# Gated mix of two linear-attention layers: a later clear for the feature weights, a fold half a V step later, and an earlier reload

## The chip, the cores and the metric

The kernel runs on one core of one Trainium2 chip. The metric is device microseconds of one execution; each comparison is the median of several runs. The core has five engines with a queue each: TensorE (PE in the profile, with its weight loads as PEld), VectorE (DVE), ScalarE (ACT), GpSimd (POOL) and SyncE (SP, which here issues nearly all DMAs). Each engine works through its own queue in order.

## The reference

Two linear-attention layers A and B read the same input x (2048 tokens, 448 features, 16 heads of 28) and are mixed by a gate:

```
def _A_ref(x, wqkv, w_phi, wo):           # _B_ref is the same with B's weights
    q, k, v = split(x @ wqkv)             # 16 heads of 28
    pq, pk = q @ w_phi, k @ w_phi         # per head, 28 x 28
    phi_q = concat(softmax(pq), softmax(-pq));  phi_k likewise
    kv = sum_s phi_k^T v;  z = sum_s phi_k
    o  = (phi_q @ kv) / (phi_q @ z + 1e-6)
    return o @ wo
g = sigmoid((x * gate_w).sum(-1))
out = g * A(x) + (1 - g) * B(x)
```

## The kernel before

**Tiles.** The 2048 tokens are 16 tiles of 128, loaded in 8 pairs. x arrives transposed, in 4 chunks of 128 feature rows. Every float32 factor is split in a high part, rounded by ACT, and a low part, the remainder, which DVE or POOL subtracts. A projection of one tile for one layer ("a half") is 11 matmuls of up to 450 columns: 4 chunks high x high, 4 high x low, 3 low x high. The letters V, K and Q name the projections: V into banks VA and VB, K into K0 and K1 and Q into Q. In the first step, V01, tiles 0 and 1 go chunk by chunk as their x and weights arrive.

**Fold.** The feature map w_phi is multiplied into the K and Q weights once, at the start. `load_wp` clears a tile wp, loads w_phi into it with eight small DMAs from POOL's queue, and subtracts its last column into wpd. Four folds F (0 to 3; layer A's two, then layer B's) multiply wpd with the raw weights wts (loaded from in_wkt and in_wqt) into the bank tile F, which there is once. After each fold DVE transposes F to SBUF (into ret for folds 0 and 2, into ru for 1 and 3; line 366), ACT rounds the high parts rk (for K) and rq (for Q), and DVE or POOL subtracts the low parts. The next fold may write F only when the transpose has read it. POOL's copy on line 350 fills a rest of wts ahead of each fold.

**Attention.** For each tile the K features are two softmaxes (ACT, DVE, POOL), and `kv` accumulates phi_k^T v for two tiles at a time in bank T (line 504). The Q features go from the bank (DVE subtracts the maximum into ru) to DRAM (qd, four DMAs of a tile) and back in another layout, then through softmaxes and a transpose into a "slot" eT. Tiles 0 to 7 are done early and spilled to DRAM (ed); tiles 8 to 15 are made just in time.

**End.** After the last kv block, N blocks (line 587) multiply phi_q of two tiles with kv; the first takes tiles 8 and 9 from slots 0 and 1, the second tiles 0 and 1 from slots 2 and 3, which `fetch` reloads from ed. Slots 2 and 3 lie in `ret` where the K features of the last tiles were, so a reload may begin only when the last kv block has read them. The gate for tiles 12 to 15 goes through DRAM (gd) into `gate` with four small DMAs. O blocks (line 635) are the output projections.

**Order.** `steps()` is the work in the order written by hand; TensorE follows it exactly. `Plan` collects every instruction as a step with an engine, an estimated cost, what it reads and writes as keys (r, w), and an `ahead` that makes it more urgent. `order()` then places the steps of the other engines, the most urgent ready step first, by those estimates. A key in r orders steps in the plan; on the chip an instruction waits for real data alone.

Of the kernel before, what the change touches and what calls it, by code (L numbers as in the profile page):

```python
# [13 lines left out]
P = 128  # L14
# [13 lines left out]
class Plan:  # L28
# [79 lines left out]

def steps():

    yield from (("V01", 0, 0, 1), ("x1",), ("V01", 1, 0, 1), ("wt", 0), ("wt", 1), ("x", 2), ("wt", 2), ("wt", 3), ("V", 2, 0), ("F", 0, "DP"), ("V", 2, 1))
    yield from (("V", 3, 0), ("F", 1, "NP"), ("V", 3, 1), ("F", 2, "DP"), ("V", 4, 0), ("F", 3, "DP"), ("x2",), ("later",), ("V", 4, 1), ("k", 0, 0), ("q", 0, 0), ("k", 0, 1), ("ks", 0))
    yield from (("K", 1), ("wo_rows",), ("q", 0, 1), ("qf", 0))
    yield from (("S", 0, JIT % 3 - 1), ("K", 2), ("Q", 1), ("S", 1, (JIT - 1) % 3 - 1), ("k", 3, 0), ("k", 3, 1), ("vm", 5, 0), ("kv", 0, 1), ("vo", 5, 0), ("ks", 3), ("V", 5, 1))
    for p in range(2, 7):
        yield "x", p + 1
        yield "K", 2 * p
        yield "Q", 2 * p - 2
        if 2 * p - 2 < JIT:
            yield "S", 2 * p - 2, (JIT - 2 * p + 2) % 3 - 1  # L120
        yield "kv", 2 * p - 2, 2 * p - 1
        yield "wo", p - 2
        if p == 3:
            yield "wo", 6
        if p < 6:
            yield "V", 2 * p + 2
        yield "K", 2 * p + 1
        yield "Q", 2 * p - 1
        if 2 * p - 1 < JIT:
            yield "S", 2 * p - 1, (JIT - 2 * p + 1) % 3 - 1  # L130
        if p < 6:
            yield "V", 2 * p + 3
        if p == 6:
            yield "gates", 0, 12
            yield "gates_b", 0, 12
    yield from (("K", 14), ("V", 14, 0), ("k", 15, 0), ("k", 15, 1), ("kv", 12, 13), ("wo", 5), ("load_wo",), ("Q", 12), ("ks", 15), ("V", 14, 1), ("V", 15, 0), ("Q", 13))
    yield from (("V", 15, 1), ("free_v",), ("free_k",), ("kv", 14, 15), ("free_e",), ("kv_turn",), ("gates", 12, NT))
    yield from (("fetch", 0, 2), ("fetch", 1, 3), ("Q", 14))
    kept, late = list(range(2, JIT - 2)), list(range(JIT, NT))
    rest = []  # L140
    while kept or late:
        rest.append((kept.pop(0) if kept else late.pop(0), late.pop(0) if late else kept.pop(0)))
    pairs = [((JIT - 1, JIT - 2), (0, 1)), ((0, 1), (2, 3))] + [(t, (2 * (i % 2), 2 * (i % 2) + 1)) for i, t in enumerate(rest)]
    for p, (tiles, slots) in enumerate(pairs):
        yield "num", tiles, slots
        if p == 0:
            yield from (("Q", 15), ("free_x",), ("free_q",))
        if p:
# [18 lines left out]
def hedgehog_mix(ctx: ExitStack, tc: tile.TileContext, xd, wv, wkt, wqt, wphi, wo, cmask, cpmask, out):  # L167
# [100 lines left out]
    def dma(o, i):  # L268
        return lambda: nc.sync.dma_start(o, i)  # L269
# [14 lines left out]
    raws = {p: (x1raw, "x1raw") if p == 1 else (xraw, "xraw") for p in range(NP)}  # L284

    def load_x0():
        for c in range(4):
            add("SP", 0.4, dma(xraw[:, c], xd[c * P:c * P + P, :2 * P]), [], [("x0raw", c)], lat=3 if c == 0 else 2, kb=131, ahead=9000.0 - 1000 * c)
            load_wv(c, 0)

    def split_x0():
# [38 lines left out]
        low_part(low, D, l, wvr[:, c, lo:hi], h.bitcast(F32), [("wvr", c, b), ("vh", c, b)], [("vl", c, b)], ahead=700.0 - 100 * c if b == 0 else 0.0)  # L330

    def load_wp():
        add("DVE", 0.15, lambda: V.memset(wp, 0.0), [], [("wp", q) for q in range(4)])
        for q in range(4):
            for b in range(2):
                i = wphi[:, b, q].rearrange("(g d) f -> d g f", g=4)
                add("POOL", 0.6, lambda q=q, b=b, i=i: G.dma_start(wp[32 * q:32 * q + DH, b], i), [("vh", 2, 0)], [("wp", q)], lat=3, two=False)
# [176 lines left out]
    def q_front(k):  # L514
        mx, km, uq, ku = qmx[k % 2], ("qmx", k % 2), uqs[k % 2], [("u", k % 2, b) for b in range(2)]

        def p4():
            return fm(bank["Q"][:, :, FO:FO + D])
        put("DVE", 2 * D, lambda: V.tensor_reduce(mx, p4(), AX.X, OP.max), ["Q"], [km])
        for b in range(2):  # L520
            put("DVE", D + 60, tt("DVE", uq[:, :, b], lambda b=b: p4()[:, b].rearrange("p (r g) f -> p r g f", r=4),
                                  mx[:, b].rearrange("p (r g) -> p r g", r=4)[:, :, :, None].to_broadcast([P, 4, 4, DH]), OP.subtract),
                ["Q", km], [ku[b]])
        m = qd[k]
        for c in range(4):
            add("SP", 0.4, dma(m[:, :, c].rearrange("r t x -> t r x"), uq[32 * c:32 * c + 32].rearrange("p r b g f -> p r (b g f)")),
                ku, [("qd", k, c)], lat=2.2, kb=160)

    def q_soft(k, slot):
        i = k % 2  # L530
# [27 lines left out]
    def gates(lo, hi):  # L558
        gl = glog[:, lo:hi]
        kl = [("gl", t) for t in range(lo, hi)]  # L560
        add("DVE", 0.1, lambda: V.tensor_scalar(gl, gl, 1.0, None, op0=OP.add), [], kl)
        add("DVE", 0.2, lambda: V.reciprocal(gl, gl), [], kl)
        add("SP", 0.4, dma(gd[:, lo:hi], gl), kl, [("gd", lo)], lat=2)
        for r in range(4):
            add("SP", 0.4, dma(gate[32 * r:32 * r + 32, 0, :, lo:hi], gd[:, lo:hi].rearrange("(c t) n -> t c n", c=4)), [("gd", lo)], [("ga", lo, r)], lat=2)

    def gates_b(lo, hi, after=()):
        add("POOL", 0.25, lambda: G.tensor_scalar(gate[:, 1, :, lo:hi], gate[:, 0, :, lo:hi], -1.0, 1.0, op0=OP.mult, op1=OP.add),
# [254 lines left out]
```

## Time and profile before

| | us |
|---|---|
| median of 3 runs | 339.39 (338.52 to 340.2) |
| the profiled execution | 338.98 |
| its span, first to last instruction | 337.2 |
| TensorE busy | 330.2 (98% of the span) |
| VectorE busy | 281.3 (83%) |
| GpSimd busy | 250.8 (74%) |
| ScalarE busy | 146.0 (43%) |

The granted TensorE clock was 0.998 of full speed. In the lines of a timeline the first number is the start in us from the start of the span, the second the duration, then engine, line, operation, destination<-sources, shapes and a count (neighbouring instructions of one kind are merged); in brackets the idle time before, and what ended it. A DMA's row is its issue, not its transfer. In a table of stretches each engine has its busy us with its number of instructions, then the granted clock, the DMA share and GB/s.

### The profile page before, as it was taken

To read this page: it belongs to the slowest core of one execution; us is meant where nothing else is said; L and a number is where in the kernel's file an instruction comes from. 1 tells how busy PE (TensorE), PEld (TensorE's weight loads), DVE (VectorE), ACT (ScalarE), POOL (GpSimd) and SP (SyncE) were. 2 spreads that over 40 slices of the span, in tenths; PEclk is the share of its full clock that TensorE was granted. 3 is DMA by queue.
4 is the path that set the end of the run, shared out by engine and by line. 5 is a ranking of instruction groups with operands and counts; after the bars stand their busy time and mean duration, and the time that the engine had idled before them with its cause. 6 is when DMAs were issued, how large, how long until landed. Compare 5 with 4: busy or idle time off the path is not lost.

```text
span 337.2 us, 8906 instructions
## 1 busy us (share of the span) xinstructions
PE 330.2 (98%) x3742; PEld 295.8 (88%) x3742; DVE 281.3 (83%) x339; ACT 146.0 (43%) x239; POOL 250.8 (74%) x210
## 2 busy tenths in 40 slices
PE   8999999999999999999999999999999999999994
PEld 7977899998999999999999999998778898888894
DVE  3648879799797896969899989796999999999860
ACT  4747845463264462524436244522133434433231
POOL 7118769999999979989896999693368868887300
PEclk9999999999999999999999999999999999999999
DMA  7983046532297857646556231855974454231011
GB/s 202 272 224 105 2 128 191 160 119 56 74 325 244 256 170 215 202 166 218 195 156 245 73 109 28 299 221 124 366 276 137 167 199 164 63 147 55 31 54 56
DMA packets 29904, 54.74 MB, mean 162 GB/s; under 512 B 4664, under 2 KB 25512, under 8 KB 27560
## 3 DMA queue, kind: packets, MB, share of 16 engines
q1 hardware_dynamic: 29608, 54.06, 49.5%
q8 instruction: 29, 0.48, 0.6%
q0 software_dynamic: 256, 0.12, 0.2%
q14 instruction: 11, 0.09, 0.1%
HBM read 31.54 MB, written 24.22 MB: 165 GB/s over the span
## 4 chain that ended last, share of the span: by engine, by line
PE 73%; DVE 10%; DMA 8%; POOL 4%; SPq 2%; issue 2%; ACT 1%; POOLq 0%; DVEq 0%; ACTq 0%
PE O L635 21%; PE K L419 14%; PE Q L419 11%; PE VA L419 8%; PE VB L419 7%; PE N L587 6%; POOL ret L263 3%; PE T L504 3%; DMA ret<-ed 2%; SPq L269 2%; DVE sm L492 2%; DMA rk<-wod 2%; DMA ret<-in_wv 1%; PE F L361 1%; PE K L451 1%
## 5 line engine op out<-in xcount | busy, mean ns | idle before, releaser
L419 PE MATMUL Q<-rq,rx 128*128 128x432 f32 x352 | 72.1, 359 | 0.0
L419 PE MATMUL K<-rk,rx 128*128 128x432 f32 x352 | 71.8, 359 | 0.0
L635 PE MATMUL O<-rk,rx 128*128 128x448 f32 x336 | 70.7, 368 | 0.4 <-issue 0.4
L635 PEld LDWEIGHTS O<-rk,rx 128*128 128x128 f32 x336 | 62.5, 188 | 8.8 <-issue 2.9
L419 PEld LDWEIGHTS Q<-rq,rx 128*128 128x128 f32 x352 | 65.8, 188 | 3.7 <-DVE ru L263 0.4
L419 PEld LDWEIGHTS K<-rk,rx 128*128 128x128 f32 x352 | 66.1, 188 | 3.1
L266 ACT ACTIVATE ret<-ret 128x896 f32<-128x896 f32 x48 | 45.6, 950 | 50.5 <-POOL ret L263 50.3
L263 POOL TENSOR_TENSOR ret<-ret,sm 128x896 f32<-128x896 f32 x32 | 53.9, 1704 | 2.4 <-DVE sm L493 2.2
L492 DVE TENSOR_REDUCE sm<-ret 128x32 f32<-128x896 f32 x32 | 33.9, 1071 | 6.5 <-ACT ret L266 6.5
L550 DVE STREAM_TRANSPOSE ret<-ret 128x2048 f32<-128x2048 f32 x16 | 36.5, 2283 | 0.8 <-POOL ret L263 0.5
L263 POOL TENSOR_TENSOR ret<-pk,mx 128x896 f32<-128x896 f32 x16 | 27.3, 1705 | 10.7 <-DVE mx L485 10.6
L545 DVE TENSOR_REDUCE qsm<-ret 128x32 f32<-128x896 f32 x32 | 33.3, 1060 | 1.6 <-ACT ret L266 1.5
L419 PE MATMUL VA<-rv,rx 128*128 128x450 f32 x154 | 34.3, 370 | 0.0
L419 PE MATMUL VB<-rv,rx 128*128 128x448 f32 x154 | 33.9, 367 | 0.0
L266 ACT ACTIVATE ret<-ru 128x896 f32<-128x896 f32 x16 | 15.3, 954 | 42.3 <-issue 20.0
L263 POOL TENSOR_TENSOR ret<-qmn,ru 128x896 f32<-128x896 f32 x16 | 28.2, 1761 | 7.2 <-DVE ret L550 4.2
L419 PEld LDWEIGHTS VB<-rv,rx 128*128 128x128 f32 x154 | 28.6, 188 | 3.5 <-issue 0.8
L419 PEld LDWEIGHTS VA<-rv,rx 128*128 128x128 f32 x154 | 28.7, 189 | 2.9 <-ACT rk L266 0.4
L263 POOL TENSOR_TENSOR ret<-ret,qsm 128x896 f32<-128x896 f32 x16 | 27.3, 1704 | 0.9
L263 POOL TENSOR_TENSOR ret<-mx,pk 128x896 f32<-128x896 f32 x16 | 27.3, 1704 | 0.7 <-DVE mx L486 0.7
L539 DVE TENSOR_REDUCE qmn<-ru 128x32 f32<-128x896 f32 x16 | 17.1, 1067 | 11.3 <-DMA ru<-qd 11.2
L607 POOL TENSOR_TENSOR rv<-rv,rd 128x896 f32<-128x896 f32 x14 | 23.9, 1704 | 1.1
(91 smaller groups left out, 448.5 us busy)
## 6 DMA issues: line engine op xcount, KB each, us to landing
ed<-ret SPq DMA_DIRECT2D x8, 1024.0 KB
ret<-ed SPq DMA_DIRECT2D x8, 1024.0 KB
qd<-ru SPq DMA_DIRECT2D x64, 112.0 KB
ru<-qd SPq DMA_DIRECT2D x16, 448.0 KB
out<-ret SPq DMA_DIRECT2D x16, 224.0 KB
wod<-wst SPq DMA_DIRECT2D x14, 224.0 KB
rk<-wod SPq DMA_DIRECT2D x2, 1568.0 KB
xraw<-in_xt SPq DMA_DIRECT2D x5, 512.0 KB
```

What stands on the lines that cost most here:

```text
L263: return lambda: ENG[eng].tensor_tensor(val(o), val(a), val(b), op)
L266: return lambda: A.activation(val(o), val(i), f, **k)
L269: return lambda: nc.sync.dma_start(o, i)
L419: nc.tensor.matmul(bank[name][:, k, lo:hi], x[:, xc, o:o + P], w[l][:, c], start=i == 0, stop=i == len(XT) - 1)
L492: put("DVE", 2 * D, lambda s=s, e3=e3: V.tensor_reduce(sm[:, s], e3, AX.X, OP.add), [ke[s], *([("u", 0, 1)] if t == 15 else [])], [("sm", ...
L504: nc.tensor.matmul(kvp()[32 * r:32 * r + DH + 1, b, g], vs[t % NV][:, b, h // 2, h % 2], es[t % NE][:, :, hs:hs + DH], start=(t == 0 and b ...
L539: put("DVE", 2 * D, lambda: V.tensor_reduce(qmn, tq.rearrange("p c b g f -> p c (b g) f"), AX.X, OP.min), [kt, *late], [kn])
L545: put("DVE", 2 * D, lambda s=s, e3=e3: V.tensor_reduce(qsm[:, s], e3, AX.X, OP.add), [ke[s], *late], [("qsm", i, s)])
L550: add("DVE", 2.25, lambda: V.transpose(eTf[slot], eq.rearrange("p s a c f -> p (s a c f)")), ke, turned(slot))
L587: nc.tensor.matmul(bank["N"][32 * g:32 * g + 32, r, 2 * b * P:2 * b * P + 2 * P], kvt[32 * r:32 * r + 32, b, s, g], eTp[slots[0] // 2][32 ...
L607: put(eng, 2 * D, lambda: ENG[eng].tensor_tensor(mid["o", n % 3].rearrange("p (c a f) -> p a c f", c=4, a=8), ctv()[:, :, i, :, :DH], rd[: ...
L635: nc.tensor.matmul(bank[pb][:, 0, :D], a, w, start=i == 0, stop=i == len(terms) - 1)
```

## The change

1. The clear of wp is placed after the low part of V-weight chunk 1 (a read of key ("vl", 1, 0)) instead of at the very start, and the eight loads of w_phi no longer name a V-weight chunk as something to come after. On the chip they wait for the clear.
2. The x chunks of tiles 0 and 1 are loaded with three DMAs (chunk 0, chunk 1, chunks 2 and 3 together) instead of four.
3. Fold 0 goes behind the second half of V for tile 2 instead of between its halves.
4. Near the end the reloads of tiles 0 and 1 stand ahead of Q 13's front, the gates and kv_turn in the written order; Q 13's stores and the last gate loads read key ("eT", 3), so that the plan places them behind the reload.

```
 def steps():
-    yield from ((...), ("V", 2, 0), ("F", 0, "DP"), ("V", 2, 1))
+    yield from ((...), ("V", 2, 0), ("V", 2, 1), ("F", 0, "DP"))
...
-    yield from ((...), ("V", 14, 1), ("V", 15, 0), ("Q", 13))
-    yield from (("V", 15, 1), ("free_v",), ("free_k",), ("kv", 14, 15), ("free_e",), ("kv_turn",), ("gates", 12, NT))
-    yield from (("fetch", 0, 2), ("fetch", 1, 3), ("Q", 14))
+    yield from ((...), ("V", 14, 1), ("V", 15, 0), ("q", 13, 0), ("q", 13, 1))
+    yield from (("V", 15, 1), ("free_v",), ("free_k",), ("kv", 14, 15), ("free_e",), ("fetch", 0, 2), ("fetch", 1, 3))
+    yield from (("kv_turn",), ("gates", 12, NT), ("qf", 13), ("Q", 14))
...
     def load_x0():
+        for c, n in ((0, 1), (1, 1), (2, 2)):
+            add("SP", 0.4, dma(xraw[:, c:c + n], xd[c * P:(c + n) * P, :2 * P].rearrange("(c p) t -> p c t", p=P)), [], [("x0raw", i) for i in range(c, c + n)], lat=3 if c == 0 else 2, kb=131 * n, ahead=9000.0 - 1000 * c)
         for c in range(4):
-            add("SP", 0.4, dma(xraw[:, c], xd[c * P:c * P + P, :2 * P]), [], [("x0raw", c)], lat=3 if c == 0 else 2, kb=131, ahead=9000.0 - 1000 * c)
             load_wv(c, 0)
...
     def load_wp():
-        add("DVE", 0.15, lambda: V.memset(wp, 0.0), [], [("wp", q) for q in range(4)])
+        add("DVE", 0.25, lambda: V.memset(wp, 0.0), [("vl", 1, 0)], [("wp", q) for q in range(4)], ahead=490.0)
...
-                add("POOL", 0.6, lambda q=q, b=b, i=i: G.dma_start(wp[32 * q:32 * q + DH, b], i), [("vh", 2, 0)], [("wp", q)], lat=3, two=False)
+                add("POOL", 0.6, lambda q=q, b=b, i=i: G.dma_start(wp[32 * q:32 * q + DH, b], i), [], [("wp", q)], lat=3, two=False)
...
     def q_front(k):
-                ku, [("qd", k, c)], lat=2.2, kb=160)
+                ku + [("eT", 3)] * (k == 13), [("qd", k, c)], lat=2.2, kb=160)
...
     def gates(lo, hi):
-            add("SP", 0.4, dma(gate[32 * r:32 * r + 32, 0, :, lo:hi], gd[:, lo:hi].rearrange("(c t) n -> t c n", c=4)), [("gd", lo)], [("ga", lo, r)], lat=2)
+            add("SP", 0.4, dma(gate[32 * r:32 * r + 32, 0, :, lo:hi], gd[:, lo:hi].rearrange("(c t) n -> t c n", c=4)), [("gd", lo)] + [("eT", 3)] * (lo > 0), [("ga", lo, r)], lat=2)
```

**VectorE at the start.** In rows of the order, rv are the split V weights, rx the split x, K a bank, zero a tile of zeros. Before:

```order
L653 MEMSET zero 128x128
L666 MEMSET K_99 128x16
L333 MEMSET wp 128x256
L666 MEMSET K_100 128x16
L338 MEMSET wpd 128x256
L263 TENSOR_TENSOR rv<-ret,rv 128x450
```

And now, where the line numbers are one higher:

```order
L667 MEMSET K_100 128x16
L339 MEMSET wpd 128x256
L263 TENSOR_TENSOR rv<-ret,rv 128x450
L263 TENSOR_TENSOR rx<-xraw,rx 128x256 x2
L263 TENSOR_TENSOR rv<-ret,rv 128x450
L263 TENSOR_TENSOR rx<-xraw,rx 128x256
L334 MEMSET wp 128x256
L263 TENSOR_TENSOR rx<-xraw,rx 64x256
L263 TENSOR_TENSOR rv<-ret,rv 128x450 x2
```

The clear of wp moved from the third place behind five subtractions, and the low part of x chunk 3 (64 rows) went ahead of that of V-weight chunk 2.

**VectorE around the folds.** The rx rows with xraw are the low parts of x tile 4, the rk rows those of the K weights (from ret: folds 0 and 2; from ru: folds 1 and 3). Before:

```order
L366 STREAM_TRANSPOSE ret<-F 128x2048
L263 TENSOR_TENSOR rk<-ret,rk 128x2x8x27 x2
L366 STREAM_TRANSPOSE ru<-F 128x2048
L263 TENSOR_TENSOR rx<-xraw,rx 64x128
L263 TENSOR_TENSOR rx<-xraw,rx 128x3x128
L366 STREAM_TRANSPOSE ret<-F 128x2048
L263 TENSOR_TENSOR rk<-ru,rk 128x2x8x27
L366 STREAM_TRANSPOSE ru<-F 128x2048
```

And now:

```order
L367 STREAM_TRANSPOSE ret<-F 128x2048
L263 TENSOR_TENSOR rx<-xraw,rx 64x128
L263 TENSOR_TENSOR rx<-xraw,rx 128x3x128
L263 TENSOR_TENSOR rk<-ret,rk 128x2x8x27
L367 STREAM_TRANSPOSE ru<-F 128x2048
L263 TENSOR_TENSOR rk<-ret,rk 128x2x8x27
L263 TENSOR_TENSOR rk<-ru,rk 128x2x8x27
L367 STREAM_TRANSPOSE ret<-F 128x2048
L367 STREAM_TRANSPOSE ru<-F 128x2048
```

The low parts of x tile 4 went from between transposes 1 and 2 to between 0 and 1, one low part of fold 0 went behind transpose 1, and the low part of fold 1 went ahead of transpose 2. On ACT the rounding of x tile 4 moved ahead of the four roundings of fold 0.

**SyncE near the end.** qd rows are stores of a Q tile (their number is the tile's), ed rows reloads of a spilled tile, ru<-qd the load of a Q tile. Before:

```order
L269 DMA ru_67<-qd12_123 128x896
L269 DMA gate_82<-gd_110 32x4x4 x2
L269 DMA qd13_124<-ru_67 32x4x224 x4
L269 DMA gate_82<-gd_110 32x4x4 x2
L269 DMA ret_66<-ed0_127 128x2048
L269 DMA ret_66<-ed1_128 128x2048
L269 DMA qd14_125<-ru_67 32x4x224 x2
```

And now:

```order
L269 DMA ru_67<-qd12_123 128x896
L269 DMA ret_66<-ed1_128 128x2048
L269 DMA ret_66<-ed0_127 128x2048
L269 DMA qd13_124<-ru_67 32x4x224 x4
L269 DMA gate_82<-gd_110 32x4x4 x3
L269 DMA ret_66<-ed2_129 128x2048
L269 DMA gate_82<-gd_110 32x4x4
L269 DMA qd14_125<-ru_67 32x4x224 x4
```

The reloads of tiles 0 and 1 went ahead of Q 13's four stores and the gates, and the reload of tile 2 went ahead of Q 14's stores.

More of the change, by code (lines that the diff above doesn't have):

```diff
@@ L109, in steps @@
 def steps():
-    yield from (("V01", 0, 0, 1), ("x1",), ("V01", 1, 0, 1), ("wt", 0), ("wt", 1), ("x", 2), ("wt", 2), ("wt", 3), ("V", 2, 0), ("F", 0, "DP"), ("V", 2, 1))
+    yield from (("V01", 0, 0, 1), ("x1",), ("V01", 1, 0, 1), ("wt", 0), ("wt", 1), ("x", 2), ("wt", 2), ("wt", 3), ("V", 2, 0), ("V", 2, 1), ("F", 0, "DP"))
     yield from (("V", 3, 0), ("F", 1, "NP"), ("V", 3, 1), ("F", 2, "DP"), ("V", 4, 0), ("F", 3, "DP"), ("x2",), ("later",), ("V", 4, 1), ("k", 0, 0), ("q", 0, 0), ("k", 0, 1), ("ks", 0))
@@ L135, in steps @@
             yield "gates_b", 0, 12
-    yield from (("K", 14), ("V", 14, 0), ("k", 15, 0), ("k", 15, 1), ("kv", 12, 13), ("wo", 5), ("load_wo",), ("Q", 12), ("ks", 15), ("V", 14, 1), ("V", 15, 0), ("Q", 13))
-    yield from (("V", 15, 1), ("free_v",), ("free_k",), ("kv", 14, 15), ("free_e",), ("kv_turn",), ("gates", 12, NT))
-    yield from (("fetch", 0, 2), ("fetch", 1, 3), ("Q", 14))
+    yield from (("K", 14), ("V", 14, 0), ("k", 15, 0), ("k", 15, 1), ("kv", 12, 13), ("wo", 5), ("load_wo",), ("Q", 12), ("ks", 15), ("V", 14, 1), ("V", 15, 0), ("q", 13, 0), ("q", 13, 1))
+    yield from (("V", 15, 1), ("free_v",), ("free_k",), ("kv", 14, 15), ("free_e",), ("fetch", 0, 2), ("fetch", 1, 3))
+    yield from (("kv_turn",), ("gates", 12, NT), ("qf", 13), ("Q", 14))
     kept, late = list(range(2, JIT - 2)), list(range(JIT, NT))
```

## The prediction

> **What bounds the kernel now.** I read the page's head first, then busy time by stretch, then TensorE's idle time.
>
> ```profile
> span 337.2 us, 8906 instructions
> PE 330.2 (98%) x3742; PEld 295.8 (88%) x3742; DVE 281.3 (83%) x339; ACT 146.0 (43%) x239; POOL 250.8 (74%) x210
> ...
> 5.40:15.40 10.00, 9.55 (x48) 8.20 (x45) 6.41 (x14) 6.61 (x15) 1.62 (x4) 1.00 1.01 302
> 22.00:36.50 14.50, 14.46 (x237) 11.30 (x236) 10.88 (x9) 12.40 (x20) 9.88 (x10) 1.00 0.43 114
> 80.00:228.00 148.00, 148.00 (x1339) 138.95 (x1340) 130.12 (x154) 66.35 (x103) 132.99 (x94) 1.00 0.57 185
> 236.00:248.00 12.00, 11.11 (x271) 8.58 (x251) 11.49 (x14) 2.74 (x5) 6.54 (x6) 1.00 0.87 305
> ```
>
> TensorE (PE, second column of a stretch) is the bound: 330.2 of 337.2 us, and 148.00 of 148 from 80 to 228. So what delays it before 80 us arrives whole at 228, and only its few idle places can give anything back. All terms are sums on TensorE's clock: where its next block starts, before and after. The profiled execution took 338.98 us; the median of the runs is 339.39, and I add the sum to that. Some 0.5% (1.7 us) is what a measurement here can tell from no change.
>
> **The start.**
>
> ```profile
> 2.05 4.80 POOL L337 DMA_DIRECT2D wp<-in_wphi  x8
> 2.11 0.43 SPq L269 DMA_DIRECT2D ret<-in_wv  x1
> 6.66 0.58 ACT L266 ACTIVATE rv<-ret 128x450 fp32r<-128x450 f32 x1 [1.41 <-DMA ret<-in_wv]
> 7.29 0.47 PE L451 MATMUL VA<-rv,rx 128*128 128x450 f32 x1 [0.45 <-ACT rv L266]
> 7.82 0.42 DVE L263 TENSOR_TENSOR rx<-xraw,rx 128x256 fp32r<-128x256 f32 x1
> 15.38 0.65 DVE L263 TENSOR_TENSOR wpd<-wp 128x216 f32<-128x216 f32 x1
> wp<-in_wphi POOLq DMA_DIRECT2D x8, 14.0 KB, 5.0
> ```
>
> The second V-weight chunk, issued at 2.11, reaches ACT at 6.66 and TensorE stands 0.45 us for it; the eight wp loads leave POOL in the same microseconds. They now start after the clear, which stands behind the subtraction of 7.82: at about 8.5. That can give back up to the 0.45. Against it, x chunks 2 and 3 travel as one 256 KB load ahead of V-weight chunk 2, which waits for 128 KB more: 0.43 us at the stretch's 302 GB/s. I take 0, bounds -0.45 and +0.45.
>
> The Trainium skill ("DMA: Bandwidth & Descriptors", Queues, rings and completion order) says each DMA engine takes packets from its queues in turn. By that, removing 8 x 14 KB from beside the weights is worth an estimated 0.37 us at 302 GB/s. The sum would be 0.37 lower; no row separates the two queues.
>
> Is wp in time? 8.5 plus 4.80 of issuing ends at 13.3; the last leaves at 12.7 and lands 5.0 later, 17.7; the subtraction's 0.65 makes 18.4. Fold 0 will want it at 20.0 (below): hidden, by 1.6 us. POOL's next work, 15.2 in this trace, is behind the issuing and is not touched.
>
> **The fold, on TensorE alone.**
>
> ```profile
> 17.75 1.97 PE L361 MATMUL F<-ret,wpd 28*32 28x256 f32 x64
> 17.91 0.40 POOL L350 COPY ret<-ret 128x256 f32<-128x256 f32 x1 [1.00 <-DMA ret<-in_wkt]
> 19.76 2.32 DVE L366 STREAM_TRANSPOSE ret<-F 128x2048 f32<-128x2048 f32 x1 [3.73 <-PE F L361]
> 21.98 2.40 PE L419 MATMUL VA<-rv,rx 128*128 128x450 f32 x11
> 24.31 1.50 PE L361 MATMUL F<-ret,wpd 28*32 28x256 f32 x64
> 25.85 2.32 DVE L366 STREAM_TRANSPOSE ru<-F 128x2048 f32<-128x2048 f32 x1 [0.47 <-PE F L361]
> 28.22 1.79 PE L361 MATMUL F<-ret,wpd 28*32 28x256 f32 x64
> 30.11 2.32 DVE L366 STREAM_TRANSPOSE ret<-F 128x2048 f32<-128x2048 f32 x1 [0.29 <-issue]
> 32.48 1.79 PE L361 MATMUL F<-ret,wpd 28*32 28x256 f32 x64
> 36.53 2.33 PE L419 MATMUL K<-rk,rx 128*128 128x432 f32 x11
> ```
>
> Fold 0 waits inside itself for POOL's copy (17.91): its transpose starts 2.01 us after it (17.75 to 19.76), fold 1's 1.54 after. A V half later the copy is done, so 0.47 us goes. Fold 0 then starts one V half (24.31 - 21.98 = 2.33) later, at about 20.0; its transpose runs from 21.54 to 23.86; fold 1, which needs the bank empty, starts at 23.9. TensorE alone would be there at 24.31 - 0.47 = 23.84. So far a gain of 0.4.
>
> **The fold, on VectorE (DVE).** Its order, and ACT's, changes most. These rows price it.
>
> ```profile
> 14.59 0.88 DVE L263 TENSOR_TENSOR rx<-ret,rx 64x128 fp32r<-64x128 f32 x2 [1.40 <-ACT rx L266]
> 18.92 0.91 SPq L269 DMA_DIRECT2D xraw<-in_xt  x2
> 22.62 1.72 ACT L266 ACTIVATE rk<-ret 128x432 fp32r<-128x432 f32 x2
> 23.60 1.77 DVE L263 TENSOR_TENSOR rk<-ret,rk 128x432 fp32r<-128x432 f32 x2 [1.53 <-ACT rk L266]
> 25.64 0.66 ACT L266 ACTIVATE rx<-xraw 128x512 fp32r<-128x512 f32 x1
> 27.74 1.34 POOL L263 TENSOR_TENSOR rq<-ret,rq 128x432 fp32r<-128x432 f32 x1
> 28.20 1.62 DVE L263 TENSOR_TENSOR rx<-xraw,rx 64x128 fp32r<-64x128 f32 x2
> 31.40 3.40 POOL L263 TENSOR_TENSOR rq<-ru,rq 128x432 fp32r<-128x432 f32 x2
> 32.34 1.22 DVE L263 TENSOR_TENSOR rk<-ru,rk 128x432 fp32r<-128x432 f32 x1
> ```
>
> Between transposes 0 and 1 stand now both low parts of x tile 4 and one low part of the K weights. The x tile's load is issued until 19.8, and ACT found it landed at 25.64; with the 4.5 us of the V-weight load above it is there near 23.5 to 24. Then ACT rounds it (0.66), to 24.2; DVE takes 0.88 for the pair, to 25.1, and 0.88 for the K part, to 26.0. Transpose 1 could start at 23.9 + 1.54 = 25.4 and starts at 26.0; it ends at 28.3, and fold 2 starts at 28.35. TensorE wanted it 3.91 after fold 1 (28.22 - 24.31): 27.8.
>
> Then the larger part. The low part of fold 1's K weights used to stand behind transpose 2 (32.34 behind 30.11) and now stands ahead of it. It needs ACT's second rounding of fold 1, 28.3 + 1.72 = 30.0, and takes 0.88; transpose 2 starts at 30.9, not at 28.35 + 1.54 = 29.9, ends at 33.2, and fold 3 starts at 33.25. That is the price with POOL out of the way. But DVE subtractions beside POOL's take longer: the x pair took 1.62 instead of 0.88 and ended at 29.82, 0.74 after POOL's 27.74 + 1.34 = 29.08; POOL's pair from 31.40 took 3.40, not twice 1.34. They run one at a time. POOL now has two of its subtractions (1.34 each) between 28 and 31, so DVE's two are moved back. If DVE goes first, POOL's second starts at 29.1, DVE's second at 30.45, and fold 3 at 33.7; if POOL goes first both times, DVE's ends at 32.6, and fold 3 starts at 35.0. I take 33.9, nearer the first, since DVE's queue is ready earlier. Before it was 32.48: **+1.4 us**, and the K block (36.53) starts that much later. Bounds: +0.4 (the x tile lands by 22.5 and POOL is out of the way) and +2.9.
>
> The Trainium skill ("SBUF — State Buffer", Who interferes with whom) has a DVE instruction with two SBUF inputs and a reading GpSimd instruction exclude each other. The rows just told agree: 0.88 against 1.62. Without it fold 3 would stand at 33.25 and the sum 0.65 lower.
>
> **The reload.**
>
> ```profile
> 78.89 1.00 PE L504 MATMUL T<-ret,vs 128*29 128x56 f32 x64 [0.21 <-POOL ret L263]
> ...
> 229.28 1.78 PE L504 MATMUL T<-ret,vs 128*29 128x56 f32 x128
> 230.99 4.60 PE L419 MATMUL Q<-rq,rx 128*128 128x432 f32 x22
> 234.45 0.85 SPq L269 DMA_DIRECT2D ret<-ed  x2
> 235.52 2.76 PE L587 MATMUL N<-ret,kvt 32*32 32x256 f32 x128
> 238.21 4.58 PE L419 MATMUL Q<-rq,rx 128*128 128x432 f32 x22
> 243.28 2.91 PE L587 MATMUL N<-ret,kvt 32*32 32x256 f32 x128 [0.50 <-DMA ret<-ed]
> 248.04 7.62 PE L635 MATMUL O<-rk,rx 128*128 128x448 f32 x36 [0.43 <-issue]
> ```
>
> A Q block lasts 4.53 us to the N block (230.99 to 235.52), so the second N block was due at 238.21 + 4.53 = 242.74 and came at 243.28: 0.54 us lost to the reload, which landed some 8.8 after its first issue (234.45). The reload overwrites what the kv block at 229.28 reads, so SP holds it until about 231, 3.4 us earlier than before, and it lands near 240: **-0.54**, with 2.7 us to spare. SP's queue stands while it waits: Q 13's four stores move from 230.2 to about 232 and share the rings with 2 MB. The next to need their buffer is Q 15's front, near 245. The gates are needed far later; Q 14's stores now wait behind the third reload, which waits for the first N block (to 238.8), about 1 us. All hidden.
>
> The stall of 0.21 at 78.89, on POOL's chain, goes when TensorE comes over a microsecond later: **-0.2** (0 if that chain moves along). The stop ahead of 248.04 has no cause in the rows; I leave it as it is.
>
> Sum: 0 + 1.4 - 0.2 - 0.54 = +0.66: 339.39 + 0.66 = **340.0 us**.
>
> **The rivals.**
> 1. Faster: VectorE is in time for transposes 1 and 2, because the x tile has landed before transpose 0 ends and ACT's roundings are early. For it: TensorE's own order gains, and ACT and DVE are idle in part of 22 to 36.5 (12.40 and 10.88 of 14.50). Against it: fold 1's second rounding cannot start before transpose 1 ends, and that is a chain, not work. Then -0.47 - 0.54 - 0.2 = -1.2: 338.2, or 337.8 with the start's best. It decides from fold 3 starting before 32.5. Chance 0.2.
> 2. POOL goes first both times: +2.5 instead of +1.4, 341.2. Chance 0.17.
> 3. The reload does not do what it says: it lands no earlier, since Q 13's and Q 12's traffic shares the rings. Then 340.6. Chance 0.1.
> 4. wp comes late, its issuing or landing slowed beside the full rings (1.01 of their time). From 1.6 us on it costs TensorE what it is late beyond that, say 1 us more: 341. Chance 0.08.
>
> **How the numbers follow.** My forecast has 0.45, and 340.0 is its time. The range, 338.2 to 341.7, runs from rival 1 to past rival 2, with the bounds of the start and of VectorE's order inside it. Faster by over 0.5% (below 337.7) needs rival 1 and the start's gain together: 0.07. Slower by over 0.5% (above 341.1): over half of rival 2, most of rival 4, the upper edge of the forecast: 0.2. Within 0.5%: 0.73.
>
> **What would show it.** Fold 0 without a gap near 20.0 and its copy long done; the wpd subtraction ended before 19; fold 1 near 23.9; transpose 1 near 26, transpose 2 not before 30.9; fold 3 at 33.3 to 35 and the first K block near 37.9; no gap at 78.89; the reload issued near 232 and no DMA wait ahead of the second N block. I am wrong if fold 3 starts before 32.5, if a new gap opens between 80 and 228, or if the second N block still waits.

## The result, and the profile after

The changed kernel takes 344.39 us (median of 6 runs, 342.75 to 344.92); the kernel before, in runs beside it and earlier, 339.31 us (6 runs, 338.36 to 340.36). The ratio is 1.0139, with a 95% interval from 1.0107 to 1.0172: 5.1 us slower, where I had forecast 0.7. A ratio here leaves out the few runs that fell in a slower state of the chip, and so can differ a little from that of the medians. The profiled execution of the changed kernel took 344.92 us, with a span of 343.1 against 337.2 before. Lines of the code have moved on by one (L504 is now L505).

The timeline of the changed kernel, TensorE and VectorE, from the start to the first K block (start, duration, engine, line, operation, tiles, count, idle time ahead and its releaser):

```profile
9.84 0.47 PE L452 MATMUL VA<-rv,rx 128*128 128x450 f32 x1 [0.40 <-DVE rv L263]
...
16.05 1.18 PE L420 MATMUL VA<-rv,rx 128*128 128x450 f32 x5
17.77 0.59 DVE L263 TENSOR_TENSOR wpd<-wp 128x216 f32<-128x216 f32 x1 [2.74 <-DMA wp<-in_wphi]
20.62 1.50 PE L362 MATMUL F<-ret,wpd 28*32 28x256 f32 x64
26.36 2.32 DVE L367 STREAM_TRANSPOSE ru<-F 128x2048 f32<-128x2048 f32 x1
30.47 1.08 DVE L263 TENSOR_TENSOR rk<-ru,rk 128x432 fp32r<-128x432 f32 x1 [0.95 <-ACT rk L266]
31.43 2.31 DVE L367 STREAM_TRANSPOSE ret<-F 128x2048 f32<-128x2048 f32 x1
33.79 1.79 PE L362 MATMUL F<-ret,wpd 28*32 28x256 f32 x64 [0.84 <-DVE ret L367]
37.84 2.33 PE L420 MATMUL K<-rk,rx 128*128 128x432 f32 x11
```

The reader sees the fold 0 stall gone (1.50 us from start to end at 20.62, 1.97 before) and paid back ahead of fold 3: the transpose at 31.43 stands behind a subtraction that waited for ACT. The first K block is 1.31 us later than 36.53. This is the number that I had worked out, though not quite by the same terms: fold 0 already begins 0.6 us later than the 20.0 that I had put.

Then the same kernel at the first kv block, with its windows (columns: length, busy us of PE, PEld, DVE, ACT, POOL with their counts, granted TensorE clock, DMA share, GB/s):

```profile
79.48 0.99 PE L505 MATMUL T<-ret,vs 128*29 128x56 f32 x64 [0.45 <-POOL ret L263]
82.80 1.72 PE L505 MATMUL T<-ret,vs 128*29 128x56 f32 x64 [2.32 <-POOL ret L263]
84.44 3.29 PE L420 MATMUL VA<-rv,rx 128*128 128x450 f32 x11
```
```profile
80.00:82.00 2.00, 0.47 (x40) 0.32 (x28) 2.00 (x3) 0.00 (x0) 2.00 (x2) 1.00 0.00 0
82.00:84.00 2.00, 1.20 (x52) 1.21 (x56) 1.55 (x3) 0.00 (x0) 2.00 (x2) 0.69 0.00 0
84.00:86.00 2.00, 2.00 (x28) 1.72 (x20) 0.58 (x1) 0.95 (x1) 2.00 (x2) 0.50 0.50 116
86.00:88.00 2.00, 2.00 (x11) 1.82 (x11) 1.78 (x3) 1.18 (x2) 2.00 (x3) 0.96 0.47 110
```

Two things are new. The second half of the kv block waits 2.32 us for POOL, and the first half 0.45 (0.21 and nothing before). And behind that pause the granted clock is 0.50, for 1.24 us of the window to 84, the 2 us to 86 and 0.16 of the last, 3.4 us in all: the 64 matmuls at 82.80 take 1.72 us for 0.99 and eleven of the V block 3.29 for some 2.5. POOL and ACT ahead of it, first in the changed kernel, then (last three rows) in the kernel before:

```profile
56.53 0.58 ACT L266 ACTIVATE wst<-wst 128x448 fp32r<-128x448 f32 x1 [2.35 <-DMA wst<-wos]
57.19 1.15 POOL L263 TENSOR_TENSOR wst<-wst 128x448 fp32r<-128x448 f32 x1 [2.44 <-ACT wst L266]
58.30 1.70 POOL L263 TENSOR_TENSOR ret<-mx,pk 128x896 f32<-128x896 f32 x1
```
```profile
53.45 0.95 ACT L266 ACTIVATE ret<-ret 128x896 f32<-128x896 f32 x1 [0.53 <-POOL ret L263]
54.11 1.70 POOL L263 TENSOR_TENSOR ret<-mx,pk 128x896 f32<-128x896 f32 x1 [0.69 <-DVE mx L486]
54.88 0.58 ACT L266 ACTIVATE wst<-wst 128x448 fp32r<-128x448 f32 x1 [0.48 <-DMA wst<-wos]
```

The step with tile `wst` is the split of the output weights wo: SP loads a piece, ACT rounds it, POOL subtracts, SP stores both. In the kernel before, POOL's first such subtraction is at 91.14, behind the kv block. In the changed kernel the planner has put it into the middle of K-soft of tile 1 (the two softmaxes of that tile's K features), and ACT's rounding ahead of an exponential; ACT waits there for the load, and POOL for ACT. POOL's next step, wanted by the kv block, starts at 58.30 instead of 54.11: 1.31 from the later K block, 1.15 for the step, 1.75 more wait (2.44 for 0.69), together 4.21.

The end of the kernel, changed:

```profile
235.59 1.26 SPq L269 DMA_DIRECT2D ret<-ed  x2
240.91 2.76 PE L588 MATMUL N<-ret,kvt 32*32 32x256 f32 x128
248.11 2.76 PE L588 MATMUL N<-ret,kvt 32*32 32x256 f32 x128
250.79 1.50 PE L636 MATMUL O<-rk,rx 128*128 128x448 f32 x6
253.87 2.41 PE L636 MATMUL O<-rk,rx 128*128 128x448 f32 x11 [1.58 <-issue]
```

The second N block no longer waits for the reload. But TensorE's unexplained stop inside the first O block, with nothing that the profile could name ("issue"), has grown from 0.43 to 1.58 us.

### The profile page after: what moved, and what is told of

Same layout as the page of the kernel before. It is cut to its first block, busy times and chain, and to the rows that moved or that the text cites. A ratio compares the mean times of both kernels' runs of the same rounds, so it can differ in the third digit from the quotient of the medians.

```text
span 343.1 us, 8905 instructions
## 1 busy us (share of the span) xinstructions
PE 331.4 (97%) x3742; PEld 296.8 (87%) x3742; DVE 281.1 (82%) x339; ACT 146.7 (43%) x239; POOL 251.4 (73%) x210
## 4 chain that ended last, share of the span: by engine, by line
PE 74%; DMA 8%; POOL 7%; SPq 4%; issue 3%; DVE 3%; ACT 0%; POOLq 0%; ACTq 0%
PE O L636 20%; PE Q L420 16%; PE K L420 14%; PE VA L420 7%; PE VB L420 6%; PE N L588 6%; POOL ret L263 5%; SPq L269 4%; PE T L505 3%; DMA ret<-in_wqt 2%; DMA ret<-in_xt 2%; DMA ret<-in_wkt 1%; DMA ret<-in_wv 1%; DVE rk L263 1%; DMA wst<-wos 1%
## 5 line engine op out<-in xcount | busy, mean ns | idle before, releaser
L420 PE MATMUL VA<-rv,rx 128*128 128x450 f32 x154 | 35.2, 377 | 0.0
L266 ACT ACTIVATE pk<-K 128x448 f32<-128x448 f32 x32 | 17.1, 539 | 24.0 <-PE K L420 24.0
```

The source lines that it names most:

```text
L266: return lambda: A.activation(val(o), val(i), f, **k)
L420: nc.tensor.matmul(bank[name][:, k, lo:hi], x[:, xc, o:o + P], w[l][:, c], start=i == 0, stop=i == len(XT) - 1)
```

## The experiments

"Pause" is below the time from the start of the last matmul of the kv block's first half to the first of its second half, and "stop" the same inside the first O block; between matmuls that follow each other at once they are 0.02 and 0.2. Before: 0.42 and 0.79; changed: 2.53 and 1.95. Pauses, stops and rows are those of one traced execution of each kernel. Times stand beside runs of the kernel before on the same chip (339.12 us for the first four, 338.89 and 338.70 for the next two fours).

**1. The folds' move alone, as the planner orders it.**

```diff
-    ... ("V", 2, 0), ("F", 0, "DP"), ("V", 2, 1))
+    ... ("V", 2, 0), ("V", 2, 1), ("F", 0, "DP"))
```

> The kernel before with one part of the change: fold 0 one V half later. In the order that the planner makes of it, POOL's subtraction for the first piece of the wo split stands inside K-soft of tile 1 again, as in the changed kernel, and ACT's second rounding of a piece and SP's load and stores for it come earlier with it. Theory A (the split moved ahead in the queues causes most of the loss, the folds the rest): first K block 0.7 to 1.3 us later than 36.53, POOL's split step near 57 with over 2 us of idle time ahead of it, a gap of 2 to 2.6 us inside the first kv block near 80, TensorE's granted clock near 0.5 for some 3 us behind the gap (1.5 us lost); 343 to 345 us. Theory B (fold order alone, the split's place does not matter): 340 to 340.7 us, no gap over 0.5 us at the kv block.

Measured: 343.56 us; ratio 1.0107 (1.0055 to 1.0160). POOL's `wst` step and the pause in its timeline:

```profile
56.01 1.16 POOL L263 TENSOR_TENSOR wst<-wst 128x448 fp32r<-128x448 f32 x1 [1.52 <-ACT wst L266]
...
81.65 1.00 PE L504 MATMUL T<-ret,vs 128*29 128x56 f32 x64 [1.94 <-POOL ret L263]
```

This part alone moves the split and makes a pause of 2.15 us. The traced execution (341.11 us) kept its clock there; the three other executions of the same kernel were granted 0.992, 0.987 and 0.993 over the whole run and took 344.24, 346.76 and 342.88.

**2. POOL's subtraction alone held back, in the changed kernel.** The key is read only by the planner.

```diff
-        put("POOL", D, tt("POOL", f[2], s[0], s[1], OP.subtract), [("ws", 0), ("ws", 1)], [("ws", 2)])
+        put("POOL", D, tt("POOL", f[2], s[0], s[1], OP.subtract), [("ws", 0), ("ws", 1)] + [("qsm", 1, 1)] * (c == 0), [("ws", 2)])
```

> The changed kernel, all its parts in, but the planner is told that POOL's subtraction for the first piece of the wo split comes after Q-soft of tile 1. So all seven pieces stand where the kernel before has them on POOL, ACT and SP. Theory A: first K block still near 37.8, but no gap over 0.3 us at the kv block near 80 and the granted clock 1.00 there; time 339.8 to 341.0 us (folds +1.3, reload -0.55, the stop inside the first O block between its old 0.8 and its new 1.95). Theory B: the gap is paid by POOL's chain starting 1.3 us later, so it stays at over 2 us and the time near 344.4. Theory C (the halved clock is a chance event and no result of the gap): clock 0.5 somewhere also here.

Measured: 341.14 us; ratio 1.0054 (1.0024 to 1.0085). The time is just over what theory A gave, but its reason was not right: the pause is still 1.84 us. Theory B, which had the pause at over 2 us, missed the time by over 3 us.

```profile
56.66 0.58 ACT L266 ACTIVATE wst<-wst 128x448 fp32r<-128x448 f32 x1 [2.50 <-DMA wst<-wos]
...
59.73 1.71 POOL L263 TENSOR_TENSOR ret<-ret,sm 128x896 f32<-128x896 f32 x1 [0.94 <-DVE sm L494]
...
81.57 1.00 PE L505 MATMUL T<-ret,vs 128*29 128x56 f32 x64 [1.62 <-POOL ret L263]
```

ACT's rounding still stood ahead of the exponential and waited 2.50 us for the load; POOL then waited for the sums that follow from the exponential. I had said that all pieces stand where they stood before, and on ACT that was not so. So experiment 5.

**3. The split moved ahead alone, in the kernel before.**

```diff
-                add("SP", 0.4, dma(wos[...], r[...]), [("q", "l", 1, 1, 2)], [("wos", c, i)], lat=3, kb=16 * n)
+                add("SP", 0.4, dma(wos[...], r[...]), [("q", "l", 1, 1, 2)], [("wos", c, i)], lat=2, kb=16 * n)
```

> The kernel before, with one number of the planner changed (landing time that it assumes for wo's rows 2 instead of 3). TensorE's order is that of before; folds, start and reload are those of before; only the first piece of the wo split moves ahead on POOL, ACT, VectorE's small steps and SP, to the place that it has in the changed kernel. Theory A: K block at 36.5 as before, but a gap of 2 to 3 us inside the first kv block near 79 and a halved clock behind it: 342.5 to 344 us. Theory B: 339.3, as before, no gap over 0.5 us.

Measured: 340.58 us; ratio 1.0042 (1.0025 to 1.0060), that is 1.4 us. It makes the pause without any change of TensorE's order:

```profile
54.80 1.15 POOL L263 TENSOR_TENSOR wst<-wst 128x448 fp32r<-128x448 f32 x1 [1.04 <-ACT wst L266]
...
80.42 0.99 PE L504 MATMUL T<-ret,vs 128*29 128x56 f32 x64 [1.41 <-POOL ret L263]
```

The pause is 1.62 us, not 2 to 3, the clock stays at 1.00, and the time is below the 342.5 to 344 that theory A gave. I had sized the pause by the changed kernel, where the load lands later (ACT there waits 2.35 us, here 0.91). Besides the split, a few softmax steps of VectorE and ACT change places in this run and in 5.

**4. The reload's move alone.**

```diff
-    ... ("V", 15, 0), ("Q", 13))
-    ... ("kv", 14, 15), ("free_e",), ("kv_turn",), ("gates", 12, NT))
-    yield from (("fetch", 0, 2), ("fetch", 1, 3), ("Q", 14))
+    ... ("V", 15, 0), ("q", 13, 0), ("q", 13, 1))
+    ... ("kv", 14, 15), ("free_e",), ("fetch", 0, 2), ("fetch", 1, 3))
+    yield from (("kv_turn",), ("gates", 12, NT), ("qf", 13), ("Q", 14))
```

> The kernel before with one part of the change: the reload of tiles 0 and 1 ahead of Q 13's stores. Only SP's queue changes. Expected by my account: the second N block starts with no DMA wait, 0.5 us earlier than 243.28; time 338.8 if the stop inside the first O block stays 0.8 us long. Rival (the stop is a fetch of instructions that takes its time from when it was asked for, so TensorE that comes earlier waits longer): the stop grows to 1.2 to 2 us and eats the half microsecond or more; 339.3 to 340.

Measured: 339.54 us; ratio 1.0016 (0.9996 to 1.0035): no gain, perhaps a loss. Second N block and first O block, and the instruction queue's row of the DMA view from 246.8 to 248.2 us (packets, MB, share of 16 engines):

```profile
243.29 2.76 PE L587 MATMUL N<-ret,kvt 32*32 32x256 f32 x128
245.97 1.49 PE L635 MATMUL O<-rk,rx 128*128 128x448 f32 x6
249.41 2.91 PE L635 MATMUL O<-rk,rx 128*128 128x448 f32 x13 [1.94 <-issue]
```
```profile
q8 instruction: 1, 0.02, 4.3%
```

The N block comes without a wait, and the stop is 2.31 us long: more than the half microsecond is gone. A 16 KB piece of instructions is being fetched just then.

**5. The split put back on POOL, ACT and SP, in the changed kernel.** As in 3, the other way round.

```diff
-                add("SP", 0.4, dma(wos[...], r[...]), [("q", "l", 1, 1, 2)], [("wos", c, i)], lat=3, kb=16 * n)
+                add("SP", 0.4, dma(wos[...], r[...]), [("q", "l", 1, 1, 2)], [("wos", c, i)], lat=6, kb=16 * n)
```

> The changed kernel, all its parts in, with one number of the planner changed the other way round (landing time that it assumes for wo's rows 6 instead of 3). TensorE's order is the changed kernel's; the first piece of the wo split stands where the kernel before has it on POOL and, other than in the run with POOL's step alone held, on ACT too, behind the exponential. Theory A (the split's place on POOL and ACT makes the pause in the kv block): first K block near 37.8; the pause is back to at most 0.5 us between matmuls there (0.42 before), the granted clock 1.00 behind it; 339.9 to 341.0 us. Theory B (POOL is late by the fold's order alone): the pause stays at 1.5 us or more, as with POOL's step alone held (1.84), and the time at 341 or above.

Measured: 340.95 us; ratio 1.0067 (1.0042 to 1.0091), where the changed kernel has 1.0139. ACT's exponential is ahead of its rounding again, and the kv block runs almost through:

```profile
55.05 0.95 ACT L266 ACTIVATE ret<-ret 128x896 f32<-128x896 f32 x1 [0.59 <-POOL ret L263]
56.38 0.58 ACT L266 ACTIVATE wst<-wst 128x448 fp32r<-128x448 f32 x1 [0.38 <-DMA wst<-wos]
...
79.24 2.08 PE L505 MATMUL T<-ret,vs 128*29 128x56 f32 x128
```

The pause is 0.31 us, and the clock 1.00 from 78 to 86. The folds, the start and the reload are all in, and the K block is no earlier (38.09), so this settles theory A against B: the place of one piece of the split costs 1.0139 - 1.0067 = 0.7% (some 2.4 us, with what the clock adds), about half of the loss; by the two intervals it is 0.3 to 1.1%.

**6 and 7. The stop: TensorE's instructions shifted, with the reload moved.**

```diff
-WARM, SMALL = 9, 14
+WARM, SMALL = 11, 0        # 6
+WARM, SMALL = 9, 34        # 7
```

> The kernel before with the reload moved, and TensorE's warm-up changed from 9 large and 14 small matmuls to 11 large ones and none small: 12 matmuls (24 instructions with their weight loads) fewer ahead of everything, so that the 16 KB pieces in which TensorE's instructions are fetched end 24 instructions later in the program. Theory F (the stop in the first O block is TensorE waiting for such a piece): the stop of 2.31 us between matmuls behind the 4th matmul of the O block is gone there, and at most a short one is left 12 matmuls later; the reload's 0.5 us then shows: 338.0 to 338.8 us. Theory G (the stop has to do with the O block's data or its place): it stays behind the 4th matmul, 2 us or more; 339.3 to 339.8 us.

> As the run with the reload moved alone, but with 34 small warm-up matmuls for 14: 20 matmuls, 40 instructions more ahead of everything. Theory F: the stop moves 20 matmuls forward in the program, out of the O block into the second N block, 16 of its 128 matmuls before its end, and is 1 to 3 us long. Theory G: it stays behind the 4th matmul of the O block.

Measured for 6: 339.71 us; ratio 1.0029 (1.0012 to 1.0046). For 7: 339.79 us, one run. The same rows as in 4, of 6:

```profile
243.65 2.75 PE L587 MATMUL N<-ret,kvt 32*32 32x256 f32 x128
246.34 5.99 PE L635 MATMUL O<-rk,rx 128*128 128x448 f32 x27
```
```profile
q8 instruction: 1, 0.02, 5.4%
```

The stop is gone in both, with data, place and reload the same and only TensorE's warm-up ahead of it changed: for theory F. In 6 the piece is fetched in the same stretch of time as in 4, but by theory F TensorE needs it 12 matmuls later and does not wait. In 7 the second half of theory F failed: no stop appeared in the N block. And the time did not fall to the 338.0 to 338.8 that theory F gave for 6. The trace of 6 shows waits for POOL and ACT of 0.27 us at a kv block near 192 and 0.33 near 231; where the rest of the saved time went is not shown.

**8. The start's two parts alone.**

```diff
-        for c in range(4):
-            add("SP", ..., dma(xraw[:, c], ...), [], [("x0raw", c)], ...)
-            load_wv(c, 0)
+        for c, n in ((0, 1), (1, 1), (2, 2)):
+            add("SP", ..., dma(xraw[:, c:c + n], ...), ...)
+        for c in range(4):
+            load_wv(c, 0)
...
-        add("DVE", 0.15, lambda: V.memset(wp, 0.0), [], [("wp", q) for q in range(4)])
+        add("DVE", 0.25, lambda: V.memset(wp, 0.0), [("vl", 1, 0)], [("wp", q) for q in range(4)], ahead=490.0)
```

> The kernel before with the start's two parts: x chunks 2 and 3 in one load ahead of the V weights' chunk 2, and the wp clear and its loads late. By my forecast nothing comes of it (0 within 0.45 us). By the traces so far the V block of tile 2 starts 0.4 to 0.6 us later than 15.41, since TensorE waits near 9.1 for chunk 2, and some of it is taken up by the waits of the folds behind it: 339.2 to 339.7 us. Rival: all of it is carried to the end, 339.7 or more.

Measured: 339.78 us; ratio 1.0022 (0.9996 to 1.0048), which does not tell the two apart.

```profile
15.84 2.41 PE L420 MATMUL VA<-rv,rx 128*128 128x450 f32 x11
...
37.00 2.33 PE L420 MATMUL K<-rk,rx 128*128 128x432 f32 x11
```

The V block of tile 2 is 0.43 later than before. The K block at 37.00 is 0.47 later than before, but only 0.1 later than in experiments 3 and 4, which have the old start and folds (36.86 and 36.90); how much of the 0.43 is left there these traces cannot tell.

**9. POOL's step done twice, in the changed kernel.**

```diff
-        put("POOL", D, tt("POOL", f[2], s[0], s[1], OP.subtract), [("ws", 0), ("ws", 1)], [("ws", 2)])
+        def sub():
+            for _ in range(1 + (c == 0)):
+                nc.gpsimd.tensor_tensor(f[2], s[0], s[1], OP.subtract)
+        put("POOL", D, sub, [("ws", 0), ("ws", 1)], [("ws", 2)])
```

> The changed kernel with POOL's subtraction for the first piece of the wo split done twice (the second writes the same values), at the place that it has there; no other engine's order changes. Theory A: POOL's chain to the kv block is 1.15 us longer and TensorE's pause there with it: 3.4 to 3.7 us between matmuls for 2.53. Theory C1 (the pause halves the clock, the more surely the longer it is): the granted clock falls to 0.5 behind the pause in the trace, and no run is granted over 0.996; 345 to 347 us. Theory C2 (the clock falls by chance): the granted clocks are spread as in the runs before, 0.996 to 1.0, and the time is 1.15 us above the changed kernel's less what its slow stretches cost, some 343.5 to 344.5 us.

Measured: 345.46 us (344.95 to 346.01); ratio 1.0193 (1.0153 to 1.0233). Granted clocks of the four runs: 0.987, 0.990, 0.987, 0.990.

```profile
80.95 0.99 PE L508 MATMUL T<-ret,vs 128*29 128x56 f32 x64 [2.03 <-POOL ret L263]
84.26 1.72 PE L508 MATMUL T<-ret,vs 128*29 128x56 f32 x64 [2.32 <-POOL ret L263]
```
```profile
82.00:84.00 2.00, 0.00 (x0) 0.00 (x0) 1.97 (x4) 0.00 (x0) 2.00 (x2) 0.57 0.00 0
84.00:86.00 2.00, 1.74 (x65) 1.59 (x65) 0.51 (x1) 0.10 (x1) 2.00 (x3) 0.50 0.27 66
86.00:88.00 2.00, 2.00 (x6) 1.78 (x7) 1.09 (x1) 1.29 (x2) 2.00 (x2) 0.50 0.48 119
88.00:90.00 2.00, 2.00 (x9) 1.81 (x8) 1.78 (x3) 0.59 (x2) 2.00 (x2) 0.72 0.22 52
```

The extra step (1.24 us more on POOL, and 0.35 more of wait ahead of it) went into the pause ahead of the first half, not into a longer one behind it: 2.03 + 2.32 for 0.45 + 2.32. The clock is halved for longer, 1.7 us of the window to 84, the next 4 us, and 1.1 us after 88. One halved stretch of 3.4 us lowers the mean clock of a run by 0.005, and the end of a traced execution by up to 0.004 more. A mean of 0.995 or less was granted to 2 of the 66 runs of the kernel before that stand beside the experiments, to 1 of 65 of experiments 4 to 8 and 10 to 12 (pauses of at most 0.99 us), 1 of 16 of experiments 2 and 3 (1.84 and 1.62), 3 of 4 of experiment 1 (2.15), 5 of 6 of the changed kernel and all 4 here. For C1, though the clock falls now and then without a long pause too.

**10. The folds' move with the split kept back.** The edits of 1 and 5 together.

> The kernel before with fold 0 one V half later, and the first piece of the wo split kept where the kernel before has it (landing time that the planner assumes for wo's rows 6 instead of 3). So of the change the order around the folds alone. First K block at 37.5 to 37.9, no pause over 0.5 us in the kv block, second N block with its old wait for the reload partly taken up; the term forecast for the folds was +1.4 less 0.2: 339.9 to 340.5 us. Rival (the folds cost nothing once the split is out of the way): 338.9 to 339.3.

Measured: 339.60 us; ratio 1.0038 (1.0015 to 1.0060), or 1.3 us.

```profile
33.33 1.79 PE L361 MATMUL F<-ret,wpd 28*32 28x256 f32 x64 [0.89 <-DVE ret L366]
...
37.38 1.93 PE L419 MATMUL K<-rk,rx 128*128 128x432 f32 x9
...
78.56 2.06 PE L504 MATMUL T<-ret,vs 128*29 128x56 f32 x128
```

The pause is 0.28 us. The K block is 0.85 later than 36.53, just below what I had put for it (37.5). The time is below the 339.9 to 340.5 that I had put, because the kernel before is at 338.70 here; the difference agrees with the forecast, +1.4 for the folds less 0.2 at the kv block. By the ratios the folds (0.38%), the start (0.22%, experiment 8) and the reload (0.16%, experiment 4) add up to 0.76%, where experiment 5, which has all three and not the split's move, has 0.67%.

**11 and 12. The shift of 24 instructions without the reload's move, and one of 12 with it.**

```diff
-WARM, SMALL = 9, 14
+WARM, SMALL = 11, 0        # 11
+WARM, SMALL = 9, 8         # 12, with the edit of 4
```

> The kernel before with only the warm-up changed, 11 large and no small matmuls for 9 and 14, the same shift by 24 instructions as with the reload moved. Theory F: the stop of 0.79 us in the first O block is gone, and small stops come in the kv blocks near 191 and 230 instead (0.27 and 0.33 us more between matmuls there). If the shift costs by these what it saves: 338.7 to 339.3 us. If it costs more than it saves, 339.5 to 340.3, then the reload did bring its half microsecond in the run with both.

> The kernel before with the reload moved, and 8 small warm-up matmuls for 14: TensorE's instructions 12 fewer ahead of everything, half the shift of before. Theory F: the stop comes 6 matmuls later in the first O block (behind the 10th) and is 1.2 us shorter than without the shift: 0.7 to 1.1 us between matmuls for 2.31; the small stops in the kv blocks near 191 and 230 stay under 0.4. With the reload's half microsecond 338.5 to 339.1 us; were it the best version, it would be under 338.5.

Measured for 11: 338.85 us; ratio 1.0010 (0.9985 to 1.0035). The second N block of 11:

```profile
243.99 2.74 PE L587 MATMUL N<-ret,kvt 32*32 32x256 f32 x128 [1.03 <-DMA ret<-ed]
```

No stop here either, but the wait for the reload is 1.03 us (0.50 before), so the two have traded places; near 191 there was no wait over 0.2, near 230 one of 0.34. For 12: 338.24 us; ratio 0.9988 (0.9968 to 1.0008). In the trace the stop is gone altogether, not shortened to 0.7 to 1.1. This is the fastest version that I measured, 0.46 us under the kernel before by the medians, and the interval does not tell it from that kernel.

## Why the prediction was wrong, and where it was right

**The step that failed: the stall at 78.89 "goes when TensorE comes over a microsecond later: -0.2 (0 if that chain moves along)".** The chain moved along and further: 2.77 us of waits at the kv block instead of 0.21. The sign that I had named for being wrong, a new gap between 80 and 228, is there at 82.80. My step took the chain of POOL as fixed in time and only TensorE as moved. But POOL's chain hangs on the folds too (its K-soft starts with the K block), and the planner, whose estimated times the folds had shifted, put the first piece of the wo split into the middle of it. This move stands in the planner's orders of POOL, ACT and SP; I priced the moves of VectorE and SP around folds and reload and no other. The price could have been read in the profile before: such a step takes POOL 1.16 us there (91.14), and the load, issued at 51.86, reaches ACT at 54.88. Experiments 3 and 5 show it in both directions: 1.4 us alone in the kernel before, some 2.4 of the changed kernel's 5.1.

**What was missing: the clock.** All rows of before show it at 1.00, and I had no term for a pause that costs more than its length. From the second half of the kv block to the next kv block TensorE took 27.33 us before and 28.83 changed:

```profile
106.22 0.99 PE L504 MATMUL T<-ret,vs 128*29 128x56 f32 x63
```
```profile
111.63 0.58 PE L505 MATMUL T<-ret,vs 128*29 128x56 f32 x29
```

That is 106.22 - 78.89 and 111.63 - 82.80: 1.5 us more for the halved clock. That the pause is its cause rests on experiment 9 and on the clocks listed there. Why 2.15 us in experiment 1 did not halve it can be read from the traces. The stretches between two changes of the clock are 3.41 and 6.83 us long at half, and 75.09, 78.51, 252.59, 256.00, 331.09 and 334.51 at full: all whole multiples of 3.41 us. So the clock changes in steps of 3.41 us, and where they lie against the program differs from run to run: a step ends at 82.74 in the changed kernel, 0.06 us ahead of the kv block's second half, and at 82.26 in experiment 1, 0.61 behind it. These two steps (columns as above):

```profile
79.33:82.74 3.41, 0.99 (x64) 0.84 (x64) 3.38 (x5) 0.00 (x0) 3.41 (x4) 1.00 0.00 0
```
```profile
78.85:82.26 3.41, 1.47 (x112) 1.32 (x112) 3.36 (x5) 0.00 (x0) 3.41 (x3) 1.00 0.00 0
```

TensorE was busy for 0.99 of 3.41 us in the one and 1.47 in the other (1.03 in experiment 9; 1.79 and 2.07 in 2 and 3, which kept their clock). In all 14 traces the clock was half behind each of the 16 steps at full clock with 1.40 us or less, one in the changed kernel, one in experiment 9 and the rest at the program's end, and full behind each of the 1344 with 1.47 or more. So what counts here is how much of a step is empty, and whether a pause falls into one step or across two is a matter of the run, which fits a clock that falls in most runs of a kernel and not in all. No run was made to test this. The Trainium skill ("TensorE: Matmul & The Clock Gate", Part 1: The HAM clock gate) has the clock halved after an idle window of about 3.4 us whose start is free-running, which would make the length of 3.4 us and the spread between runs plain. The 3.4 us agree with the traces, but the windows here were not idle: they held 0.99 and 1.03 us of matmuls. Its section HAM oscillation warns of idle gaps over 3.4 us; here a gap of 2.32 us was enough, with 0.45 and a block of short matmuls ahead of it.

**Another: "the stop ahead of 248.04 has no cause in the rows; I leave it as it is".** The wait grew by 1.15 us in the profiled execution (0.43 to 1.58). In the runs with the reload moved and TensorE's instructions in their old place it is 1.95 (changed), 1.95 (2), 2.31 (4), 1.83 (5) and once nothing (9); with the reload in its old place 0.79 (before), 0.25, 0.51, 0.81 and 0.52 (1, 3, 8, 10). In all four runs with TensorE's instructions shifted it is gone. And in all nine traces with a stop TensorE goes on 1.26 to 1.47 us after a 16 KB packet of the instruction queue has ended; in 9, which has none, it had ended 1.83 us before that matmul. So the stop is tied to the fetch of a piece of instructions, right behind an N block of 256 instructions in 2.7 us. The account is not complete: it had a stop in the N block in 7 and a shorter one in 12, and there was neither. The Trainium skill ("Runtime: NRT & Kernel Launch", Instruction fetch mechanics) calls crossing such a border mostly hidden; here it was not, by up to 1.9 us of waiting. With the reload in its old place the fetch starts 2.0 to 2.4 us after the second N block does, with the reload moved 3.2 to 3.9 (1.2 in 9). Why it comes later is open: the transfers beside it differ, but no run changed them alone.

**The reload: right as a mechanism, not as a term.** It was issued 1.1 us after 234.45 although TensorE was 5.4 us later, and the second N block no longer waits: -0.54 as worked out. What I had not seen is that the stop right behind it grows by more than that, and the measured term is +0.5 us by the ratio (experiment 4; -0.1 to +1.2 by its interval) instead of -0.54.

**The folds: right as a mechanism, the number in part by luck.** Forecast were fold 3 at 33.9 and the first K block near 37.9; measured 33.79 and 37.84, by the mechanism named, the subtraction that waits for ACT ahead of transpose 2 (30.47, then 31.43). But of the forecast 0.65 us were POOL's, on top of the 33.25 "with POOL out of the way", and with the folds alone (experiment 10) fold 3 starts at 33.33. There VectorE's subtraction began before POOL's (29.98 and 30.22) and took 1.12 us for 0.88. In the changed kernel fold 0 began 0.6 us late by the start, and that filled the place of the 0.65. The folds' own part at the K block is 0.85 us in experiment 10 and 1.18 in experiment 1.

**The start: its sum was mis-sized.** The wp loads were in time, as worked out (the subtraction ended at 18.36; I had 18.4). What made TensorE wait 0.40 us at 9.84 was VectorE: it clears wp at 8.40 and subtracts x chunk 3 at 8.70 (0.42 us) ahead of the low part of V-weight chunk 2 at 9.15, an order that I had listed and not priced. Tile 2's V block came 0.64 later, outside my 0.45. What is left of it at the end, experiment 8 cannot tell from nothing (ratio 1.0022, from 0.9996).

For the profiled executions the parts are 1.31 (to the K block) + 2.56 (more wait at the kv block) + 1.50 (clock) - 0.56 (reload) + 1.15 (stop) = 5.96; their spans differ by 5.9 (differences of up to 0.2 elsewhere cancel).

## What to carry to other kernels

Where a planner orders the engines, a shift early in the program moves steps that have nothing to do with the edit: go through the order of every engine down to the next place where the bound engine waits, and price each step that has moved into a chain which that place hangs on, a wait for a transfer above all. A step put into a chain with no slack costs its duration and its own wait, and a pause of two microseconds on TensorE can cost half as much again when the clock falls behind it, as it did here in most runs. Where the bound engine is stopped by nothing that the profile names, find out what it is before counting on time saved just ahead of it.

## What the runs showed of the hardware

- TensorE's granted clock fell to 0.50 for 3.4 us behind waits of 0.45 and 2.32 us with 0.99 us of short matmuls between them, and for about 6.8 us behind 2.03 and 2.32. It did not in the traces with single pauses of 1.62, 1.84 and 2.15 us. In these traces it changed in steps of 3.41 us, and fell behind every full-clock step in which TensorE was busy for 1.40 us or less, and behind none with 1.47 or more.
- A stop of up to 1.9 us in a stream of matmuls with nothing named to wait for ended 1.26 to 1.47 us after a 16 KB packet of the instruction queue, in nine traces, and was gone in the four kernels with 12 to 40 instructions added or taken away at the program's start.
- Kernels with the same start and folds started the first K block up to 0.4 us apart (36.53, 36.86 and 36.90).
